# Order of sums, parts and raw loads in the q/k projection of a gated attention and expert kernel

## The chip, the cores and the metric

The kernel runs on one core of a Trainium2 chip. The metric is device time in microseconds (us); the median of three runs of the kernel before is 1882.5 (1881.57 to 1883.23). Engines are named as the profile names them: PE (TensorE), ACT (ScalarE), DVE (VectorE), POOL (GpSimd) and SP (SyncE, which here only issues DMAs). Each engine takes its instructions in its own program order.

## The reference

```
x: (2048, 1024)
gate = sigmoid(sum(x * gate_w))                      # one number a token
a    = attention(x @ wqkv, 32 heads of 32) @ wo
b    = peer(x, w_q, k1, k2, u, v)                    # each of 32 heads picks one of 64 experts
out  = gate * a + (1 - gate) * b
```

All of it is float32. This case touches the first stage: q and k, which are `x @ wqkv` for 2 x 1024 columns, the gate's sums `x * gate_w`, and a fold of `w_q` with the keys that the router of `b` needs.

## The kernel before, in words

**Split products.** A float32 operand is split into a high part (ACT copies it into a rounded type) and a low part (DVE subtracts the high part from it); `split` (L93) does both. A product is then three matmuls for each 128 rows of depth: high x high, high x low, low x high. So whatever PE multiplies must first have gone through ACT and then DVE.

**Two passes, sixteen units.** The tokens are taken in two passes of 1024. A pass has eight units; a unit makes 128 columns of q and 128 of k for the 1024 tokens. The two column blocks and two halves of the depth make a 2 x 2 matrix of weights (A11, A12, A21, A22), the two token blocks and two halves of the depth a 2 x 2 matrix of x (B11 to B22). The first unit of a pass, 0 and 8, is *plain*: eight block products, 96 matmuls, in four PSUM banks (7, 0, 1 and 2). The other seven use seven block products instead of eight (`FACTORS`, L258): P1 = A11 B11, P5 = S1 T1, P6 = S2 T2, P2 = A12 B21, P7 = S3 T3, P3 = S4 B22, P4 = A22 T4, in this order, 12 matmuls each, in banks 0 to 5 in turn. S1 to S4 are sums of weight blocks, made anew for each unit (`w_sum`, L200), T1 to T4 sums of x blocks, made once a pass (`x_sum`, L137). Sums are made on DVE and in place: T1 overwrites raw B11, T3 raw B12, T2 raw B22, T4 raw B21. `w_parts` and `x_quarter` split them. An x sum or split is 128 x 2048 elements ("wide" in what follows), a weight sum, split or evacuation 128 x 512 ("narrow"). The parts of x of a pass also have places that others leave: T2 takes the place of B12's parts, T3 that of raw B22, T4 that of raw B11 and B12 (`PASS`, L101).

**Evacuation.** `evac` (L224) splits a finished block of q or k; later (`run_late`, L215) ACT squares it, which frees the PSUM bank, and issues two stores. The plain units evacuate their four banks while the next unit runs.

**Side work.** `gate_sums` (L173) multiplies all raw x of a pass with the gate's column, 64 PE instructions of 256 columns, copies the four results on ACT into the tile that also holds raw B22, and stores them from POOL's queue. `fold` (L290) multiplies two tiles' worth of `w_q` with key differences (`kpad`), and asks for the next four tiles of 512 KB; after every second fold ACT copies the bank, and in the next unit `fold_t` (L310) transposes the copy on PE, right after P1. It runs at the end of a unit, and in three units after P2 too.

**Order.** All of it stands in the order written out in `unit` (L432): after each product a hook (work put there by name, `hooks`) and then one step of the preparation of the next unit. At the passes' start the order is written out around the plain products (L371 to L404, and L527 to L553) and in `after_plain` (L410). SP issues loads in the order of the program: `load_w` (1 MB, the weights of the unit after the next) at a unit's start, wq tiles at its end, and raw x of the second pass in units 5 and 7 (`next_raw`, L507). Tiles are reused, so a load waits until the last reader of its tile is done, and a store or load also until the transfer that used its semaphore before it is done.

**Unit 15**, the last, splits the router's folded weights between its products (`split_wp`, L586), two buffers deep: the split of one frees the buffer for the load of the one after the next. Router tiles on PE follow it.

Of the kernel before, what the change touches and what calls it, by code (L numbers as in the profile page):

```python
# [31 lines left out]
def gated_mha_peer_kernel(ctx, tc, xT, wqkv, wv, wo, wq, k12, ug, v, out):  # L32
# [81 lines left out]
    def bank_at(i):  # L114
        return ps1.tile([128, 512], F32, name=f"bk{i}")
# [57 lines left out]
    def gate_sums(p):  # L173
        pz = bank_at(6)
        for kc in range(KC):
            for q in range(4):
                nc.tensor.matmul(pz[32 * q:32 * q + 1, :256], gw[:, kc, :], x_raw_at(kc, 256 * q),
                                 start=(kc == 0), stop=(kc == KC - 1))
        for q in range(4):
            row = slice(32 * q, 32 * q + 1)  # L180
            nc.scalar.activation(XR["zs"][row, :], pz[row, :256], AF.Copy)
            c = TOK0[p] + 256 * q
            dma(ZD[:, c:c + 256], XR["zs"][row, :], nc.gpsimd)

# [91 lines left out]
    def load_wq(n):  # L276
        for half in range(2):
            t = wqp.tile([128, 2, 512], F32, name="wqt", bufs=4)
            dma(t, wq[n // 4, n % 4][:, half * 1024:(half + 1) * 1024].rearrange("p (a m) -> p a m", a=2))
            wq_t[n, half] = t  # L280

    def kpad_diffs():
        nc.vector.memset(kpad, 0.0)
        for i in range(4):
            nc.vector.tensor_tensor(out=kpad[:, :, i, 7 * i:7 * i + 7], in0=kraw[:, :, 1:],
                                    in1=kraw[:, :, 0:1].to_broadcast([128, 2, 7]), op=OP.subtract)

    fold_ps, fold_no, pending = [], [0], []

    def fold():  # L290
# [12 lines left out]
        if i == 3:  # L303
            wt = ev.tile([128, 512], F32, name="u4", bufs=1)
            nc.scalar.activation(wt, ps, AF.Copy)
            pending.append((n // 4, wt))
        for m in range(n + 1, min(n + 3, 32)):
            load_wq(m)

    def fold_t():  # L310
        if not pending:
# [55 lines left out]
        nc.tensor.matmul(b0[1, 1][:, :128], ident, ident, start=True, stop=True)  # L367
    dma(gw, ug.rearrange("p (k m) -> p k m", k=KC)[:, :, 64:65], nc.gpsimd)
    dma(kraw, k12.rearrange("p (a e) -> p a e", a=2), nc.gpsimd)

    for kc in range(KC):  # L371
# [35 lines left out]
    def plain_evac(u, w, n):  # L407
        evac(w, CHUNK[u], TOK0[u // KC] // 512 + n, b0[w, n], b0[w, n])

    def after_plain(u, done):  # L410

        rest = [(w, n) for n in range(2) for w in range(2) if (w, n) not in done]
        p, v = u // KC, u + 1
        x_quarter(p, "T2")
        plain_evac(u, *rest.pop(0))
        w_parts(v, "A12")
        plain_evac(u, *rest.pop(0))
        first, second = rest[:1], rest[1:]
        hooks[v, "P1"] = [(plain_evac, u, *a) for a in first] + [(w_parts, v, "S3")]
        hooks[v, "P5"] = [(x_quarter, p, "T3"), (w_parts, v, "A22")]  # L420
        hooks[v, "P6"] = [(x_quarter, p, "T4")] + [(plain_evac, u, *a) for a in second] + [(load_w, u + 3)]

    hooks = {}
    after_plain(0, ())
    load_w(2)
    fold()
    FOLDS = {1, 2, 3, 4, 5, 6, 8, 9, 10, 11, 12, 13}
# [4 lines left out]
    def unit(u):  # L432
        p, c, v = u // KC, CHUNK[u], u + 1
        n0 = TOK0[p] // 512
        seven = v < NUNIT and v != KC
        def ready(name, f=w_parts, *args):
            if seven:
                w_parts(v, name)

        def hook(name):  # L440
            for f, *a in hooks.pop((u, name), []):
                f(*a)

        def place(name):
            return ev.tile([128, 512], F32, name=name, bufs=1)

        def add(out, a, b):
            nc.vector.tensor_tensor(out=out, in0=a, in1=b, op=OP.add)  # L448
# [9 lines left out]
        if seven:  # L458
            w_sum(v, "S1")
            w_sum(v, "S3")  # L460
        ready("A11")
        p5 = product("P5")
        ready("S1")
        if seven:
            w_sum(v, "S2")
        hook("P5")
        p6 = product("P6")
        u2, u4 = place("u2"), place("u4")
        add(u2, c1, p6)
        add(u4, u2, p5)  # L470
        ready("S2")
        if seven:
            w_sum(v, "S4")
# [6 lines left out]
        ready("A12")  # L480
        hook("P2")
        p7 = product("P7")
        u7 = place("u7")
        add(u7, u4, p7)
        add(u2, u2, p7)
        evac(1, c, n0 + 1, u7, p7)
        ready("S3")
        hook("P7")
        p3 = product("P3")
        add(u4, u4, p3)  # L490
        evac(0, c, n0 + 1, u4, p3)
        ready("S4")
        hook("P3")
        p4 = product("P4")
        add(u2, u2, p4)
        evac(1, c, n0, u2, p4)
        ready("A22")
        hook("P4")
        if u in FOLDS:
            fold()  # L500

    def load_a21():
        t = wr.tile([128, 2, KC, 128], F32, name="wraw")
# [3 lines left out]
    def next_raw(which):  # L507
# [4 lines left out]
        else:  # L512
            load_quarter(0 if which == "r21" else 1, 1, XR["B21" if which == "r21" else "B22"])

    hooks[5, "P1"] = [(next_raw, "r21")]
# [12 lines left out]
    load_w(KC + 2)  # L528
    gate_sums(1)
    for ki, n in ((0, 0), (0, 1), (1, 0), (1, 1)):  # L530
        for w in range(2):
            for k in range(HC):
                for i in range(3):
                    plain_mm(w, n, ki * HC + k, i, ki == k == i == 0, ki == 1 and k == HC - 1 and i == 2)
        nxt = KC + 1
        if (ki, n) == (0, 0):
            x_sum(1, "T1")
            x_quarter(1, "T1")
        elif (ki, n) == (0, 1):
            for name in ("S1", "S3"):  # L540
                w_sum(nxt, name)
            w_parts(nxt, "A11")
            w_parts(nxt, "S1")
            w_sum(nxt, "S2")
            w_parts(nxt, "S2")
            for name in ("T3", "T2", "T4"):
                x_sum(1, name)
        elif (ki, n) == (1, 0):
            for w in range(2):
                plain_evac(KC, w, 0)  # L550
            w_sum(nxt, "S4")
            w_parts(nxt, "S4")
    after_plain(KC, ((0, 0), (1, 0)))  # L553
    fold()


# [1116 lines left out]
```

## Time and profile before

| what | us |
|---|---|
| runs of the kernel before, median | 1882.5 |
| the profiled execution, its own time | 1882.36 |
| the span of its profile | 1880.6 |
| opening, up to the first fold on PE | 36.57 |
| router's first tile to the end (starts at) | 413.2 |
| PE busy in the span | 1835.0 |
| DVE busy in the span | 1470.5 |

A timeline row has start, length, engine, line, operation, output<-inputs, shapes and a count; in brackets stand the idle time ahead of it and the instruction that ended it. Rows of equal instructions that follow each other are merged. A name such as `xh` stands for all tiles called xh0, xh1 and so on: `xh`, `xl` and `x` are tiles of x, `A` and `S` parts of weights, `bk` the PSUM banks, `hi` and `lo` the parts of evacuated q and k, `wraw` raw weights, `wqt` raw `w_q`, `wpr` and `wph` the router's weights. PE's row lengths overlap a little, so the distance between starts is the better measure of a product.

### The profile page before, as it was taken

To read this page: it belongs to the slowest core of one execution; us is meant where nothing else is said; L and a number is where in the kernel's file an instruction comes from. 1 tells how busy PE (TensorE), PEld (TensorE's weight loads), DVE (VectorE), ACT (ScalarE), POOL (GpSimd) and SP (SyncE) were. 2 spreads that over 40 slices of the span, in tenths; PEclk is the share of its full clock that TensorE was granted. 3 is DMA by queue.
4 is the path that set the end of the run, shared out by engine and by line. 5 is a ranking of instruction groups with operands and counts; after the bars stand their busy time and mean duration, and the time that the engine had idled before them with its cause. 6 is when DMAs were issued, how large, how long until landed. Compare 5 with 4: busy or idle time off the path is not lost.

```text
span 1880.6 us, 26511 instructions
## 1 busy us (share of the span) xinstructions
PE 1835.0 (98%) x10083; PEld 1106.0 (59%) x10083; DVE 1470.5 (78%) x1276; ACT 1315.2 (70%) x1730; POOL 182.7 (10%) x224
## 2 busy tenths in 40 slices
PE   8799889999999999999999999999999999999999
PEld 6577666777888854444444444444444444447787
DVE  5766486668987878888888888888888888896674
ACT  3544354452143379999999999999999999994221
POOL 0000000006710110000000000000000000000000
PEclk9899989999999999999999999999999999999999
DMA  7587658855027778676777777777877777776861
GB/s 247 184 257 272 218 143 280 295 158 196 2 88 249 257 196 183 155 178 150 174 177 169 172 167 180 166 184 164 186 167 178 156 174 179 172 160 174 290 182 56
DMA packets 136977, 344.98 MB, mean 183 GB/s; under 512 B 18320, under 2 KB 60080, under 8 KB 117712
## 3 DMA queue, kind: packets, MB, share of 16 engines
q1 hardware_dynamic: 97120, 193.41, 34.3%
q0 software_dynamic: 17904, 112.10, 27.7%
q10 hardware_dynamic: 21824, 37.76, 6.5%
q8 instruction: 80, 1.31, 0.3%
q14 instruction: 49, 0.40, 0.1%
HBM read 171.50 MB, written 72.10 MB: 130 GB/s over the span
## 4 chain that ended last, share of the span: by engine, by line
PE 66%; DVE 3%; DMA 3%; POOL 1%; issue 1%; ACT 1%; SPq 0%; DVEq 0%; ACTq 0%; POOLq 0%
PE ring L1220 27%; PE o L1241 25%; PE pa L868 6%; PE bk L868 6%; PE ring L1254 1%; POOL eq L655 1%; DMA accd<-P 1%; DMA out<-rb 1%; DMA accd<-rd 1%; PE pa L1432 1%; DVE eq L664 0%; DMA smd<-ssb 0%; DVE mm L662 0%; DVE vt L95 0%; DVE m L649 0%
## 5 line engine op out<-in xcount | busy, mean ns | idle before, releaser
L1230 ACT ACTIVATE P<-ring 128x1024 f32<-128x1024 f32 (+2 forms) x1031 | 912.6, 985 | 14.7 <-DMA accd<-P 2.2
L1270 DVE TENSOR_TENSOR acc<-acc,P 128x2048 f32<-128x2048 f32 x319 | 731.0, 2291 | 75.1 <-ACT P L1230 49.4
L1241 PE MATMUL o<-P,V 128*32 128x512 f32 x3840 | 464.8, 599 | 0.0
L1220 PE MATMUL ring<-Q,K 98*128 98x512 f32 x1024 | 272.3, 407 | 0.2 <-ACT P L1230 0.2
L1220 PE MATMUL ring<-z,z 98*128 98x512 f32 x1020 | 270.7, 407 | 0.6 <-ACT accd L1230 0.6
L1220 PEld LDWEIGHTS ring<-Q,K 98*128 98x128 f32 x1024 | 181.8, 188 | 144.9 <-ACT P L1230 73.4
L1220 PEld LDWEIGHTS ring<-z,z 98*128 98x128 f32 x1020 | 181.3, 188 | 143.0 <-ACT P L1230 72.3
L1241 PEld LDWEIGHTS o<-P,V 128*32 128x32 f32 x3840 | 98.8, 109 | 223.1 <-issue 213.9
L1263 POOL DMA_DIRECT2D accd<-P x95 | 81.5, 858 | 930.4 <-ACT P L1230 364.0
L1268 DVE TENSOR_TENSOR acc<-P,P 128x2048 f32<-128x2048 f32 x32 | 73.4, 2293 | 73.4 <-ACT P L1230 73.4
L267 PE MATMUL bk<-xh,S 128*128 128x512 f32 x336 | 88.8, 419 | 18.4 <-ACT xh L94 8.9
L267 PEld LDWEIGHTS bk<-xh,S 128*128 128x128 f32 x336 | 67.7, 204 | 36.0 <-ACT xh L94 9.7
L267 PE MATMUL bk<-xl,S 128*128 128x512 f32 x336 | 82.6, 398 | 1.9 <-DVE xl L95 1.8
L267 PE MATMUL bk<-xh,A 128*128 128x512 f32 x336 | 83.0, 396 | 1.1 <-DVE A L95 1.1
L267 PEld LDWEIGHTS bk<-xh,A 128*128 128x128 f32 x336 | 62.0, 188 | 25.2 <-issue 10.1
L94 ACT ACTIVATE hi<-u 128x512 fp32r<-128x512 f32 x42 | 26.5, 632 | 69.4 <-DVE u L448 66.3
L267 PEld LDWEIGHTS bk<-xl,S 128*128 128x128 f32 x336 | 63.6, 191 | 18.0 <-DVE xl L95 2.1
L1273 DVE TENSOR_TENSOR acc<-acc,accd 128x2048 f32<-128x2048 f32 x32 | 73.1, 2285 | 0.0
L1230 ACT ACTIVATE accd<-ring 128x1024 f32<-128x1024 f32 (+2 forms) x64 | 62.3, 1034 | 2.0 <-PE ring L1220 1.9
L868 PE MATMUL pa<-woh,acc 128*128 128x512 f32 x192 | 62.2, 389 | 0.0
L95 DVE TENSOR_TENSOR A<-wraw,A 128x512 fp32r<-128x512 f32 (+2 forms) x47 | 31.3, 667 | 34.3 <-ACT A L94 33.3
L94 ACT ACTIVATE xh<-xh 128x512 fp32r<-128x512 f32 (+1 forms) x25 | 24.2, 986 | 39.5 <-DVE xh L850 20.0
(286 smaller groups left out, 2176.1 us busy)
## 6 DMA issues: line engine op xcount, KB each, us to landing
accd<-P POOLq DMA_DIRECT2D x95, 1024.0 KB, 7.6
wqt<-in_wq SPq DMA_DIRECT2D x64, 512.0 KB
wraw<-in_wqkv SPq DMA_DIRECT2D x28, 512.0 KB
qdh<-hi ACTq DMA_DIRECT2D x32, 256.0 KB
qdl<-lo ACTq DMA_DIRECT2D x32, 256.0 KB
kdh<-hi ACTq DMA_DIRECT2D x32, 256.0 KB
kdl<-lo ACTq DMA_DIRECT2D x32, 256.0 KB
z<-kdh SPq DMA_DIRECT2D x32, 256.0 KB
```

The source lines that it names most:

```text
L94: nc.scalar.activation(hi, src, AF.Copy)
L95: (on or nc.vector).tensor_tensor(out=lo, in0=src, in1=hi.bitcast(F32), op=OP.subtract)
L267: nc.tensor.matmul(ps, a[i][:, k, :], b[j][:, k, :], start=(k == 0 and i == j == 0), stop=(k == HC - 1 and i == 1))
L655: nc.gpsimd.tensor_tensor(out=eq, in0=eq, in1=e8[:, None, :].to_broadcast([128, 64, 8]), op=OP.mult)
L868: nc.tensor.matmul(ps, self.a[a][i][:, k, :], self.b[b][j][k], start=(not first and k == 0 and i == j == 0), stop=(k == HC - 1 and i == 1))
L1220: on_ring(nc.tensor.matmul(ring[:, i, :], K[:98, kt * 128:(kt + 1) * 128], Q[:98, qc * 512:(qc + 1) * 512], start=True, stop=True), i)
L1230: on_ring(nc.scalar.activation(P[h, kt][:, q0 * 512:(q0 + m) * 512].rearrange("p (a m) -> p a m", a=m), ring[:, i:i + m, :], AF.Exp, scale ...
L1241: nc.tensor.matmul(O[h][32 * qc:32 * qc + 32, :], Vt[g][:, kt, 32 * j:32 * j + 32], p[:, qc * 512:(qc + 1) * 512], start=(kt == 0), stop=( ...
L1263: nc.gpsimd.dma_start(ACCD[h], P[h, kt], accum_op=OP.add)
L1268: nc.vector.tensor_add(ACC[h], P[h, 0], P[h, kt])
L1270: nc.vector.tensor_add(ACC[h], ACC[h], P[h, kt])
L1273: nc.vector.tensor_add(ACC[h], ACC[h], ACCD[h])
```

## The change

What it does, in the order of the program:

- The gate's product is cut in two: the half that reads B11 and B12 comes ahead of the fifth of eight plain steps in the first pass (`kc == HC`), the other half ahead of the last; its bank is 5 instead of 6; its copies and stores (`gate_out`) come later, behind S2's parts.
- The key differences `kpad` are made on POOL right after their load, not on DVE in the middle of the plain steps.
- S1, S3 and S1's parts of unit 1 leave the sixth plain step. The preparation at the end of the first pass's plain unit is now T1, T3's sum, S1, S3, A11, T2, S2, gate copies, T4's sum; then A12, one evacuation, T3, S3, and in unit 1 another evacuation, S4, T4, A22 and the last two evacuations.
- In the second unit of a pass (1 and 9) the preparation of the next unit moves from P1 and later to P2 and later, and its A22 into the next unit's P1 (`turns`).
- `load_w` moves from a unit's start to behind P6, and raw x in unit 7 is asked for ahead of it. The fold of unit 6 no longer asks for wq tiles; the start of the second pass does (`load_wqs`).
- In unit 7 the splits of the second pass go B21, B11, B12, A21, B22 instead of B11, B12, A21, B21, B22, and the preparation during the second plain unit is reordered as in the first.
- In unit 15 the eight splits of the router's weights go two, one, one, two, one, one over P1 to P3, instead of one at each and two at P4.

```diff
+    pz = []
+    def gate_mm(kcs):
+        if kcs[0] == 0:
+            pz[:] = [bank_at(5)]
+        for kc in kcs:
             for q in range(4):
...
+    def gate_out(p):
         for q in range(4):
...
     def kpad_diffs():
-        nc.vector.memset(kpad, 0.0)
+        nc.gpsimd.memset(kpad, 0.0)
...
-        if kc == 5:
-            w_sum(1, "S1")
-            w_sum(1, "S3")
-            w_parts(1, "S1")
-            kpad_diffs()
+        if kc == HC:
+            gate_mm(range(HC))
         if kc == KC - 1:
-            gate_sums(0)
+            gate_mm(range(HC, KC))
             x_sum(0, "T1")
             x_quarter(0, "T1")
+            x_sum(0, "T3")
+            for name in ("S1", "S3"):
+                w_sum(1, name)
+            w_parts(1, "S1")
             w_parts(1, "A11")
+            x_sum(0, "T2")
+            x_quarter(0, "T2")
             w_sum(1, "S2")
             w_parts(1, "S2")
-            w_sum(1, "S4")
-            w_parts(1, "S4")
-            for name in ("T3", "T2", "T4"):
-                x_sum(0, name)
+            gate_out(0)
+            x_sum(0, "T4")
...
-    after_plain(0, ())
+    w_parts(1, "A12")
+    plain_evac(0, 1, 0)
+    x_quarter(0, "T3")
+    w_parts(1, "S3")
+    hooks[1, "P1"] = [(plain_evac, 0, 0, 1), (w_sum, 1, "S4"), (w_parts, 1, "S4")]
+    hooks[1, "P5"] = [(x_quarter, 0, "T4"), (w_parts, 1, "A22")]
+    hooks[1, "P6"] = [(plain_evac, 0, 1, 1), (plain_evac, 0, 0, 0)]
...
+        turns = (dict(P2=("S1+", "S3+", "A11"), P7=("S1", "S2+", "S2"), P3=("S4+", "A12"), P4=("S3", "S4"))
+                 if u % KC == 1 else
+                 dict(P1=("S1+", "S3+", "A11"), P5=("S1", "S2+"), P6=("S2", "S4+"), P2=("A12",),
+                      P7=("S3",), P3=("S4",), P4=("A22",)))
...
-        if v + 1 < NUNIT and u % KC != 1 and v + 1 != KC:
-            load_w(v + 1)
...
         hook("P6")
+        ready("P6")
+        if v + 1 < NUNIT and v + 1 != KC:
+            load_w(v + 1)
...
         if u in FOLDS:
-            fold()
+            fold(u != KC - 2)
...
-    hooks[7, "P2"] = [(x_quarter, 1, "B11")]
-    hooks[7, "P7"] = [(x_quarter, 1, "B12")]
-    hooks[7, "P3"] = [(w_parts, 8, "S4", "A21"), (x_quarter, 1, "B21")]
+    hooks[7, "P2"] = [(x_quarter, 1, "B21")]
+    hooks[7, "P7"] = [(x_quarter, 1, "B11")]
+    hooks[7, "P3"] = [(x_quarter, 1, "B12"), (w_parts, KC, "S4", "A21")]
...
     plain_banks(1)
-    load_w(KC + 2)
-    gate_sums(1)
+    load_wqs()
+    gate_mm(range(KC))
+    x_sum(1, "T1")
+    x_quarter(1, "T1")
+    x_sum(1, "T3")
+    run_late()
...
         if (ki, n) == (0, 0):
             for name in ("S1", "S3"):
                 w_sum(nxt, name)
+            w_parts(nxt, "S1")
+            gate_out(1)
+            for name in ("T2", "T4"):
+                x_sum(1, name)
+        elif (ki, n) == (0, 1):
+            x_quarter(1, "T2")
             w_parts(nxt, "A11")
             w_sum(nxt, "S2")
             w_parts(nxt, "S2")
+            x_quarter(1, "T3")
+            w_parts(nxt, "S3")
+            w_sum(nxt, "S4")
+            w_parts(nxt, "S4")
+            x_quarter(1, "T4")
+        else:
+            plain_evac(KC, 1, n)
+            if n:
+                w_parts(nxt, "A12")
+            plain_evac(KC, 0, n)
+    load_w(KC + 2)
...
-    for kc, name in enumerate(("P1", "P5", "P6", "P2", "P7", "P3", "P4")):
-        hooks[15, name] = [(split_wp, kc)]
+    for name, kcs in (("P1", (0, 1)), ("P5", (2,)), ("P6", (3,)), ("P2", (4, 5)), ("P7", (6,)), ("P3", (7,))):
+        hooks[15, name] = [(split_wp, kc) for kc in kcs]
     hooks[15, "P6"].append((split_n1,))
-    hooks[15, "P4"].append((split_wp, 7))
```

More of the change, by code (lines that the diff above doesn't have):

```diff
@@ L171, in x_raw_at @@
         return XR[f"B{1 + kc // HC}{1 + n}"][:, kc % HC, c:c + 256]
-    def gate_sums(p):
-        pz = bank_at(6)
-        for kc in range(KC):
+    pz = []
[3 more added lines that the diff above has]
+        for kc in kcs:
             for q in range(4):
-                nc.tensor.matmul(pz[32 * q:32 * q + 1, :256], gw[:, kc, :], x_raw_at(kc, 256 * q),
+                nc.tensor.matmul(pz[0][32 * q:32 * q + 1, :256], gw[:, kc, :], x_raw_at(kc, 256 * q),
                                  start=(kc == 0), stop=(kc == KC - 1))
+    def gate_out(p):
         for q in range(4):
             row = slice(32 * q, 32 * q + 1)
-            nc.scalar.activation(XR["zs"][row, :], pz[row, :256], AF.Copy)
+            nc.scalar.activation(XR["zs"][row, :], pz[0][row, :256], AF.Copy)
             c = TOK0[p] + 256 * q
@@ L280, in load_wq, with load_wqs, fold @@
             wq_t[n, half] = t
+    def load_wqs():
+        n = fold_no[0]
+        for m in range(n, min(n + 2, 32)):
+            load_wq(m)
     def kpad_diffs():
-        nc.vector.memset(kpad, 0.0)
+        nc.gpsimd.memset(kpad, 0.0)
         for i in range(4):
-            nc.vector.tensor_tensor(out=kpad[:, :, i, 7 * i:7 * i + 7], in0=kraw[:, :, 1:],
+            nc.gpsimd.tensor_tensor(out=kpad[:, :, i, 7 * i:7 * i + 7], in0=kraw[:, :, 1:],
                                     in1=kraw[:, :, 0:1].to_broadcast([128, 2, 7]), op=OP.subtract)
     fold_ps, fold_no, pending = [], [0], []
-    def fold():
+    def fold(load=True):
         for _ in range(2):
@@ L306, in fold @@
             pending.append((n // 4, wt))
-        for m in range(n + 1, min(n + 3, 32)):
-            load_wq(m)
+        if load:
+            load_wqs()
     def fold_t():
@@ L408, in plain_evac @@
         evac(w, CHUNK[u], TOK0[u // KC] // 512 + n, b0[w, n], b0[w, n])
[L410 to L421, printed above, removed]
-    hooks = {}
-    after_plain(0, ())
+    hooks = {}
+    w_parts(1, "A12")
[5 more added lines that the diff above has]
+    hooks[1, "P6"] = [(plain_evac, 0, 1, 1), (plain_evac, 0, 0, 0)]
     load_w(2)
@@ L435, in unit, with ready @@
         seven = v < NUNIT and v != KC
[L436 to L438 removed]
+        turns = (dict(P2=("S1+", "S3+", "A11"), P7=("S1", "S2+", "S2"), P3=("S4+", "A12"), P4=("S3", "S4"))
+                 if u % KC == 1 else
+                 dict(P1=("S1+", "S3+", "A11"), P5=("S1", "S2+"), P6=("S2", "S4+"), P2=("A12",),
+                      P7=("S3",), P3=("S4",), P4=("A22",)))
+        def ready(name):
+            if not seven:
+                return
+            for part in turns.get(name, ()):
+                if part[-1] == "+":
+                    w_sum(v, part[:-1])
+                else:
+                    w_parts(v, part)
         def hook(name):
@@ L457, in unit @@
         hook("P1")
[L458 to L461, printed above, removed]
+        ready("P1")
         p5 = product("P5")
-        ready("S1")
-        if seven:
-            w_sum(v, "S2")
         hook("P5")
+        ready("P5")
         p6 = product("P6")
@@ L479, in unit @@
             fold()
-        ready("A12")
         hook("P2")
+        ready("P2")
         p7 = product("P7")
```

25 lines of the change are left out of this document (9 added, 16 removed).

## The prediction

> **What bounds the kernel now.** I read the windows by stage first, then the TensorE timeline where those show it idle, then the VectorE, ScalarE and SyncE timelines there. The stages are: opening, first pass up to the second folded unit, the rest of that pass, and the same cuts of the second pass.
>
> ```profile
> span 1880.6 us, 26511 instructions
> ...
> 36.57:88.05 51.48, 36.92 (x158) 26.09 (x158) 39.80 (x46) 26.35 (x47) 0.81 (x1) 0.87 0.58 173
> 88.05:208.74 120.69, 120.69 (x578) 90.98 (x577) 71.65 (x111) 49.76 (x105) 2.27 (x3) 1.00 0.82 272
> 208.74:292.80 84.06, 67.06 (x318) 47.75 (x318) 58.80 (x62) 41.92 (x68) 2.78 (x5) 0.88 0.56 175
> ```
>
> The columns are length, busy time of PE, PEld, DVE, ACT, POOL, then granted clock, DMA share and GB/s. From P2 of unit 2 to the end of unit 7 PE is busy all 120.69 us: nothing that other engines do there can be gained. In the two stages after the plain products PE idles 14.6 and 17.0 us and its clock falls to 0.87 and 0.88. Idle time plus slow clock, 14.6 + 0.13 x 36.9 and 17.0 + 0.12 x 67.1, is 44 us: the ceiling of any reordering here. The change lives in these two stages and in unit 15.
>
> ```profile
> 20.38 6.30 PE L255 MATMUL bk<-xl,A 128*128 128x512 f32 x26
> 30.06 1.91 PE L177 MATMUL bk<-xh,gw 128*1 128x256 f32 x32
> ...
> 51.02 0.80 PE L267 MATMUL bk<-xh,S 128*128 128x512 f32 x1 [5.50 <-ACT xh L94]
> 53.54 4.49 PE L267 MATMUL bk<-xh,S 128*128 128x512 f32 x11 [1.73 <-DVE xh L95]
> 66.98 4.82 PE L267 MATMUL bk<-xh,S 128*128 128x512 f32 x12 [6.23 <-ACT bk L222]
> ...
> 82.11 0.62 PE L317 MATMUL bk<-ident,u 128*128 128x128 f32 x4
> 85.33 2.88 PE L267 MATMUL bk<-xh,S 128*128 128x512 f32 x12
> ```
>
> P6 of unit 1 waits for T2's parts, P7 for T3's and for an evacuated bank. A product of 12 matmuls takes 2.72 (85.33 to 88.05), but 4.8 after a long wait: each stall costs some 2 us beyond itself. In the second pass the same comes with waits for raw x, S4, T2 and the fold's copy:
>
> ```profile
> 213.66 0.38 PE L177 MATMUL bk<-xl,gw 128*1 128x256 f32 x2 [1.48 <-DMA xl<-in_xT]
> ...
> 223.94 4.84 PE L255 MATMUL bk<-xh,S 128*128 128x512 f32 x12 [5.44 <-ACT S L94]
> ...
> 256.06 0.80 PE L267 MATMUL bk<-xh,S 128*128 128x512 f32 x1 [3.40 <-ACT xh L94]
> 262.70 2.90 PE L267 MATMUL bk<-xl,A 128*128 128x512 f32 x12
> 285.20 0.66 PE L317 MATMUL bk<-ident,u 128*128 128x128 f32 x4 [2.50 <-ACT u L305]
> 285.61 7.34 PE L267 MATMUL bk<-xh,S 128*128 128x512 f32 x24
> ```
>
> Behind these waits stands one serial chain that crosses DVE and ACT. Its steps:
>
> ```profile
> 32.01 2.29 DVE L142 TENSOR_TENSOR xh<-xh 128x2048 f32<-128x2048 f32 x1 [3.06 <-PE bk L177]
> 37.31 2.29 DVE L95 TENSOR_TENSOR xl<-xh,xl 128x2048 fp32r<-128x2048 f32 x1 [3.01 <-ACT xl L94]
> 44.28 4.68 DVE L142 TENSOR_TENSOR xh<-xh,xh 128x2048 f32<-128x2048 f32 x2
> 54.01 0.68 DVE L95 TENSOR_TENSOR A<-wraw,A 128x512 fp32r<-128x512 f32 x1
> 54.60 0.68 DVE L95 TENSOR_TENSOR lo<-bk,hi 128x512 fp32r<-128x512 f32 x1
> ...
> 33.76 1.57 ACT L181 ACTIVATE xh<-bk 1x256 f32<-1x256 f32 x4 [6.60 <-PE bk L177]
> 35.36 1.92 ACT L94 ACTIVATE xl<-xh 128x2048 fp32r<-128x2048 f32 x1
> 51.48 0.62 ACT L94 ACTIVATE A<-wraw 128x512 fp32r<-128x512 f32 x1
> 52.00 0.59 ACT L94 ACTIVATE hi<-bk 128x512 fp32r<-128x512 f32 x1
> ```
>
> DVE takes 2.2 a wide step and 0.60 a narrow one (54.01 to 54.60); ACT 1.85 and 0.52 to 0.6. DVE began T1's sum only at 32.01, because it overwrites raw x that the gate product, last in PE's order, still had to read; T1's high part then stood behind ACT's four gate copies (3.01 lost); and the sums T3, T2, T4 (44.28 on) stood ahead of T2's parts, which P6 needs first.
>
> **First pass, part by part.** No matmul is added or removed, so what counts is when things come due. I lay the new order out by hand with these steps, each engine in its own order. The gate's first half (16 matmuls of the row at 30.06, which with its second half is 3.5, so 1.75) now runs on PE ahead of the fourth block, 20.4 to 22.15, and frees B11 and B12. S1, S3 and the kpad work leave DVE's queue ahead of the last x splits, so DVE is free at about 22. T1: sum 22.2, high part 24.5, low part done 28.6. T3's sum to 30.8, S1 and S3 to 32.0, their and A11's low parts to 33.3, T2's sum to 35.5 (the second gate half is read by 32.1), its high part to 37.4, low part to 39.6; S2 is whole at 41.4. PE ends the plain products at 20.4 + 4 x 2.72 + 3.5 = 34.8, folds to 36.7 (kpad now comes from POOL, a few small instructions with 15 us and more of cover; were it late, the fold waits), and P1, P5, P6 follow without a stall to 44.9.
>
> Then come new waits. P2 writes bank 0, which needs (1,0) evacuated and squared. On ACT that square stands behind S2, the gate copies (now 40.8 to 42.4), A12, the bank's own split, and T3's high part, which overwrites the tile that holds the gate sums and so waits for their four stores:
>
> ```profile
> zd<-xh POOLq DMA_DIRECT2D x4, 1.0 KB, 1.5
> ...
> 232.24 1.97 POOL L76 DMA_DIRECT2D zd<-xl  x4 [34.14 <-ACT xl L181]
> ```
>
> 0.5 an issue and 1.5 to land put it at 44.6; with S3, c1's copy and the square, bank 0 is free at 48.2. PE waits 3.4 and runs slow: P2 48.2 to 52.7. P7 needs bank 1, squared after T4's high part: 54.7; it ends at 59, P3 62, P4 64.7, fold 66.5, unit 2's P1 69.3. So PE is 12 us ahead there, but DVE isn't: it is busy without a gap from 55 on with four plain evacuations, unit 1's own and all of unit 2's preparation. The fold's copy stands on ACT behind S3 and S4 of that list, at 72.5; unit 2's transposes start at 73.1 (a new stall of 3.8), P5 runs slow to 78.0, P6 ends at 80.8. Before it ended at 88.05. **First pass: -7.2 us.** The bounds: without the new stall at the transposes -11, and -4 if each step of the ACT/DVE chain loses another 0.1 (some 30 steps from 41 to 73).
>
> Moving load_w behind P6 costs nothing: SP doesn't wait for P6, it issues as before once the buffer's last split is done, and only loads in between go first.
>
> **Second pass.** Positions are given on the clock of the profile, that is, without the 7.2 already won.
>
> ```profile
> 201.41 0.63 ACT L94 ACTIVATE hi<-c 128x512 fp32r<-128x512 f32 x1 [4.35 <-DVE c L448]
> 211.25 1.91 ACT L94 ACTIVATE xh<-xh 128x2048 fp32r<-128x2048 f32 x1 [9.22 <-DMA xh<-in_xT]
> ...
> 188.18 2.07 SPq L76 DMA_DIRECT2D wqt<-in_wq  x4
> 193.00 5.74 SPq L76 DMA_DIRECT2D wraw<-in_wqkv  x2
> 198.84 2.07 SPq L76 DMA_DIRECT2D xh<-in_xT  x4
> 202.09 0.38 SPq L76 DMA_DIRECT2D xl<-in_xT  x1
> ```
>
> ACT stood 9.22 in unit 7 for raw x, which was queued behind four wq and two w loads: 5 MB from 188.18 to 211.25, 4.6 us per MB. Now raw x issues when P1 of unit 7 frees its tile (191.9, six products and the transposes before the unit's end at 208.6): 2 MB land at 201, the other 1 MB at 206, w(9) at 210, the wq loads at 219. Meanwhile ACT splits B21, which is long there: 202.0 to 203.9, low part to 206.1. Then, with unit 7's evacuations between: B11 whole at 212.2, B12 218.2, A21 218.8, B22 224.8. PE ends unit 7 at 208.6, finds raw x landed, gate to 212.1, B11 x A11 to 214.9, waits 3.9 for A21 (S4's slot), slow to 223.4, and ends the plain products at 239.6. DVE and ACT, without a gap: T1 whole at 231, S1 235.2, T2 241.8, A11 242.4, S2 244.3, T3 247.7, S3, S4 250.1, T4 253.6, evacuations and A12 257.4. So PE folds to 241.5, P1, P5, P6 to 250.7, then waits 6.7 for A12 and starts P2 at 257.4; before it was 262.70. P2 slow to 262, P7, P3, P4 to 270.3, fold 272.2, P1 of unit 10 275.1. The fold's copy is on ACT at 276.3 by the same count as in unit 2, so transposes start at 277.0 against 285.20. Both are followed by the same slow start. **Second pass: -8.2 us**, bounded by -5.3 (what P2 shows, if the later part of the chain gains nothing) and -12 (if the wait for A12 shrinks to that for S2).
>
> **Unit 15.** The splits of the router's weights move up a slot, two in P1 and P2.
>
> ```profile
> 404.22 0.58 ACT L94 ACTIVATE wph<-wpr 128x448 fp32r<-128x448 f32 x1 [2.86 <-DMA wpr<-wpd]
> 420.55 0.50 PE L641 MATMUL bk<-wph,xl 128*128 128x512 f32 x1 [1.75 <-ACT wph L94]
> 430.82 0.63 DVE L649 TENSOR_REDUCE m<-bk 128x64 f32<-128x448 f32 x1 [1.47 <-ACT xu L645]
> ```
>
> A load lands some 3.6 after the split that frees its buffer, so the sixth and seventh can't come before 416.8 and 417.6: ACT waits there with evacuations queued behind it. The last split comes at 421 instead of 422, PE's first tile gains 2 us, but the last evacuation is 3 later and DVE starts its router steps 1.5 later, which its own 1.47 of idle at 430.82 takes up. I take 0, with -2 and +3.
>
> **Sum**: -7.2 - 8.2 + 0 = -15.4. The profiled execution took 1882.36, its span 1880.6 and 1.76 around it; the median shown is 1882.5, so both agree. 1882.5 - 15.4 = 1867. From unit 2 to the end the work is unchanged and PE busy, so the gain passes through.
>
> **Two rules of the Trainium skill.** The row: after a wait of only 2.50 the next 24 matmuls took 7.34 instead of 5.44 (285.61). The Trainium skill, TensorE: Matmul & The Clock Gate, What's actually happening, says the clock halves only after an idle window of about 3.4 us. By that rule my stalls of 1.9, 3.4 and 3.9 might cost no slow clock, and an estimate from that page is some 4 us more gain, 1863; the trace shows the slow rate, but after shorter waits too, so the sum keeps the rows.
>
> The row for POOL's stores: four issues in 1.97 while DVE ran these:
>
> ```profile
> 231.72 2.29 DVE L95 TENSOR_TENSOR xl<-xl,xl 128x2048 fp32r<-128x2048 f32 x1 [1.73 <-ACT xl L94]
> 233.93 2.29 DVE L142 TENSOR_TENSOR xh<-xh 128x2048 f32<-128x2048 f32 x1
> ```
>
> The Trainium skill, SBUF — State Buffer, two separate sides, speaks against this change: DMAs issued from POOL starve while DVE holds the port pair that they share. That is the third rival.
>
> **Rivals.** (1) *DVE's total sets the end.* The new order only removes idle time ahead of T1, some 6 us (3.06 + 3.01) in the first pass, and PE's lead is paid back in units 2 and 10: half the gain, 1875. For it: DVE had 39.8 of 51.5 busy; against: the chain above already counts DVE without gaps. (2) *Slower: ACT's stores stand behind loads.* ACT's issue of a store waits for the load that last held its semaphore, and what is behind it on ACT waits too, as here in unit 10:
>
> ```profile
> 287.71 0.54 ACT L320 ACTIVATE u<-bk 128x448 f32<-128x448 f32 x1 [1.47 <-DMA wqt<-in_wq]
> ```
>
> In unit 7 two stores stand behind raw x's last piece and the last two wq loads, which are now queued behind raw x. At 4.6 us per MB they land at 206 and 219.5, and ACT gets there at 207.4 and 220.7: 1.3 to spare. At twice that, 9.2 us per MB, the last lands at 247 and B22's split and all behind it come 26 late: 1882.5 - 7.2 - 8.2 + 26 = 1893. It decides from 7.4 us per MB. Against: the rate of 188 to 211 held with stores running too. (3) *POOL's gate stores are held* for a DVE step each: 4 x 2.3 instead of 1.97, T3 7 us later in the first pass; the second has 5 us of room: 1867 + 7 + 2 = 1876. Against: the 1.97. (4) *The transposes don't stall* and the clock recovers: -11 - 12 = 1859.
>
> **Chances.** Forecast 0.58, (1) 0.15, (2) 0.08, (3) 0.07, (4) 0.12. A difference under 0.2%, 3.8 us, can't be told from none here. Slower than that is (2) with 0.01 of (1), 0.09; no change is 0.05 of (1), where PE's whole lead is paid back; faster is the rest, 0.86. The range takes in (4) and (3): 1857 to 1876.
>
> **What would show it.** Right: P6 of unit 1 starts within 0.5 us of P5's end; a wait of 3 to 4 before P2 by a square (bank 0); transposes of unit 2 near 73 with a wait for the fold's copy; gate sums of the second pass without a DMA wait; B21 split while raw x lands; P2 of unit 9 waiting 5 to 8 for A12. Wrong: a store on ACT that waits past 208 on the second pass, T3 more than 3 us behind the gate copies, or PE idle in units 2 to 7.

## The result, and the profile after

The changed kernel takes 1871.27 us (median of five, 1868.22 to 1874.19) against 1882.5 (median of five, 1879.4 to 1883.96): ratio 0.9942, 95% interval 0.9926 to 0.9958. The gain is 11.2 where 15.4 was forecast. Run again beside other kernels it took 1870.59 against 1883.61, ratio 0.9932 (0.9918 to 0.9945). The profiled execution is the fastest of its five, 1868.22 with a span of 1866.5, so its span shows 14.1 of gain, 3 more than the medians.

The windows by stage of the changed kernel (length, busy time of PE, PEld, DVE, ACT, POOL, then granted clock, DMA share, GB/s). The first starts at P1 of unit 1 (the one before started a fold earlier; from P1 it was 49.63 long), the second at P2 of unit 2, the third at the second gate sum and ends at P2 of unit 10:

```profile
36.67:82.62 45.95, 35.09 (x144) 26.10 (x141) 32.98 (x42) 25.70 (x49) 2.78 (x5) 0.89 0.70 210
82.62:203.65 121.03, 121.03 (x578) 91.00 (x577) 75.37 (x113) 53.64 (x110) 2.27 (x3) 1.00 0.80 265
203.65:280.79 77.14, 63.15 (x317) 46.03 (x317) 54.32 (x58) 38.19 (x64) 2.78 (x5) 0.91 0.60 182
```

Between the two passes PE is still busy throughout, 121.03 of 121.03. Where it idled, the old waits are gone and others stand in other places, less in sum: 10.9 instead of 14.6 in the first stage, 14.0 instead of 17.0 in the third. The third stage is 6.9 shorter, so more than half of that, 3.9, are matmuls that ran faster (granted clock 0.91 instead of 0.88). PE's timeline of the changed kernel, first pass:

```profile
42.90 3.04 PE L272 MATMUL bk<-xh,S 128*128 128x512 f32 x12 [0.46 <-ACT xh L186]
49.21 3.02 PE L272 MATMUL bk<-xl,A 128*128 128x512 f32 x12 [3.27 <-ACT bk L227]
55.80 5.49 PE L272 MATMUL bk<-xh,S 128*128 128x512 f32 x12 [3.57 <-ACT bk L227]
...
75.18 1.12 PE L327 MATMUL bk<-ident,u 128*128 128x128 f32 x4 [3.55 <-ACT u L315]
75.95 4.12 PE L272 MATMUL bk<-xl,S 128*128 128x512 f32 x12
```

P6 starts half a microsecond behind P5's end (it stood 7.2 before). P2 and P7 now wait for squares of the banks that they write, the transposes of unit 2 for the fold's copy. The second pass of the changed kernel, same view:

```profile
203.65 1.91 PE L180 MATMUL bk<-xh,gw 128*1 128x256 f32 x32
...
211.89 0.73 PE L260 MATMUL bk<-xh,S 128*128 128x512 f32 x2 [1.67 <-ACT S L94]
214.30 4.14 PE L260 MATMUL bk<-xh,S 128*128 128x512 f32 x10 [1.67 <-DVE S L95]
...
253.10 5.49 PE L272 MATMUL bk<-xl,A 128*128 128x512 f32 x12 [6.80 <-ACT A L94]
...
274.82 0.66 PE L327 MATMUL bk<-ident,u 128*128 128x128 f32 x4 [2.84 <-ACT u L315]
275.24 5.72 PE L272 MATMUL bk<-xh,S 128*128 128x512 f32 x24
```

The gate sum no longer waits for raw x; A21 costs 3.3 in two pieces, A12 6.80. Starts of the same steps on PE in six profiled executions (the last two kernels come below):

| kernel | P2 of unit 2 | P4 of unit 7 | P2 of unit 10 | P4 of unit 15 | router's wait for DVE | span |
|---|---|---|---|---|---|---|
| before | 88.05 | 205.92 | 292.78 | 410.33 | 470.31 | 1880.6 |
| changed | 82.62 | 200.83 | 280.79 | 398.33 | 457.16 | 1866.5 |
| first pass only | 83.87 | 201.73 | 288.86 | 406.59 | 468.01 | 1879.2 |
| second pass only | 87.59 | 206.45 | 287.73 | 405.29 | 466.66 | 1876.3 |
| all reordered | 70.78 | 196.91 | 266.37 | 386.37 | 445.32 | 1855.6 |
| the same, stores on POOL | 68.99 | 188.21 | 254.94 | 376.91 | 434.08 | 1845.6 |

In the changed kernel 5.4 comes up to unit 2, nothing (118.2 against 117.9) up to unit 7, 6.9 up to unit 10, nothing up to unit 15, 1.1 in the router; behind it 1409.3 follow against 1410.3. Of the 5.4, 1.8 stand before the first fold on PE already (it starts at 34.81 against 36.57), and that start varies by 2.3 from run to run, as the last section shows.

### The profile page after: what moved, and what is told of

Its sections match the earlier page's. It is cut to its first block, busy times and chain, and to the rows that moved or that the text cites. A ratio compares the mean times of both kernels' runs of the same rounds, so it can differ in the third digit from the quotient of the medians.

```text
span 1866.5 us, 26507 instructions
## 1 busy us (share of the span) xinstructions
PE 1827.8 (98%) x10083; PEld 1105.7 (59%) x10083; DVE 1467.8 (79%) x1271; ACT 1316.1 (71%) x1730; POOL 183.7 (10%) x229
## 4 chain that ended last, share of the span: by engine, by line
PE 64%; issue 6%; DVE 2%; POOL 2%; DMA 1%; ACT 0%; POOLq 0%; DVEq 0%; ACTq 0%; SPq 0%
PE ring L1239 28%; PE o L1260 25%; PE pa L887 6%; PE pa L1444 2%; PE ring L1273 1%; POOL eq L674 1%; PE pa L1451 1%; DVE eq L683 0%; DVE mm L681 0%; DMA t1l<-xl 0%; DVE m L668 0%; DVE xh L893 0%; DMA vd<-xh 0%; DMA xl<-in_wo 0%; DVE m L669 0%
## 5 line engine op out<-in xcount | busy, mean ns | idle before, releaser
L1239 PEld LDWEIGHTS ring<-Q,K 98*128 98x128 f32 x1024 | 182.0, 188 | 144.0 <-ACT P L1249 73.1
L272 PE MATMUL bk<-xh,S 128*128 128x512 f32 x336 | 83.0, 400 | 4.0 <-ACT bk L227 3.6
L272 PEld LDWEIGHTS bk<-xh,S 128*128 128x128 f32 x336 | 64.2, 193 | 19.1 <-ACT bk L227 4.0
L1292 DVE TENSOR_TENSOR acc<-acc,accd 128x2048 f32<-128x2048 f32 x32 | 73.1, 2284 | 0.0
L272 PE MATMUL bk<-xl,A 128*128 128x512 f32 x168 | 43.1, 408 | 10.1 <-ACT A L94 6.8
```

The lines of the kernel that those rows point to most:

```text
L272: nc.tensor.matmul(ps, a[i][:, k, :], b[j][:, k, :], start=(k == 0 and i == j == 0), stop=(k == HC - 1 and i == 1))
L1239: on_ring(nc.tensor.matmul(ring[:, i, :], K[:98, kt * 128:(kt + 1) * 128], Q[:98, qc * 512:(qc + 1) * 512], start=True, stop=True), i)
L1292: nc.vector.tensor_add(ACC[h], ACC[h], ACCD[h])
```

## The experiments

**One pass at a time.** The second pass alone (everything up to unit 6 as before), then the first alone (everything from unit 7 on as before):

```diff
-        if kc == HC:
-            gate_mm(range(HC))
+        if kc == 5:
+            w_sum(1, "S1")
+            w_sum(1, "S3")
+            w_parts(1, "S1")
...
```
```diff
-    load_wqs()
+    load_w(KC + 2)
     gate_mm(range(KC))
-    x_sum(1, "T1")
...
+    gate_out(1)
...
```

> Only the first pass is as changed (gate sum in two halves, the new order of sums and parts, unit 1's turns, kpad from POOL, weights asked for behind P6 up to unit 6); unit 7, its loads, the second pass and unit 15 are as before. Theory (the two passes gain apart from each other, each by the order in which ACT and DVE make its operands): P6 of unit 2 ends near 82.6 as in the changed kernel, 5.4 before the old 88.05, nothing is lost up to the end, 1882.5 - 5.4 = 1877. Rival (DVE's total decides and the lead is paid back in the units behind): 0, 1882. Rival (all of the 11 to 14 us comes from raw x being there earlier in the second pass): 0, 1882.

> Only unit 7 with its loads, the second pass and its turns are as changed; the first pass and unit 15 are as before. Theory: the distance from the end of unit 7 to P2 of unit 10 shrinks from 84.0 to 77.1, so -6.9, 1875.6. Rival (the second pass gains only because the first hands it a lead): 0, 1882. Rival (what the first pass gains is given back and the second pass makes all of it): -12, 1870.

Measured: 1878.77 (ratio 0.9982, 0.9973 to 0.9991) and 1876.31 (0.9966, 0.9957 to 0.9976) against 1882.55: -3.8 and -6.2. The table shows each lead arise in its own pass and last up to P4 of unit 15 (3.7 and 5.0 there). Behind it the router's stretch differs from run to run: of the first pass's lead the span of its profile, the slowest of eleven runs, keeps 1.4. Neither is a condition of the other, and neither is the whole: together they make 10.0, without unit 15.

**Unit 15 as before.**

```diff
-    for name, kcs in (("P1", (0, 1)), ("P5", (2,)), ("P6", (3,)), ("P2", (4, 5)), ("P7", (6,)), ("P3", (7,))):
+    for kc, name in enumerate(("P1", "P5", "P6", "P2", "P7", "P3", "P4")):
...
```

> The changed kernel, but unit 15's splits of the router's weights in the slots of before. Theory (unit 15's part is worth what lies between the end of P4 of unit 15 and the row where PE waits for DVE in the router: 57.1 before, 55.95 after): +1.1, 1872.4. My forecast had 0 for it, 1871.3. Rival (the spread of these runs hides it): within 0.5 of the changed kernel.

Measured 1873.38 (0.9945, 0.9932 to 0.9959), 2.1 and 2.8 above the changed kernel's two medians. From P4 of unit 15 to the router's wait it takes 59.67 (399.41 to 459.08), against 58.83 with the change. The intervals of the ratios overlap (0.9945 against 0.9942 and 0.9932), so the times alone don't settle it; the positions are on the side of a gain of 1 to 2, not of my 0.

**Raw x not ahead.**

```diff
+        if u == KC - 1:
+            load_w(v + 1)
...
-            fold(u != KC - 2)
+            fold()
...
-    load_wqs()
```

> The changed kernel, but the loads around unit 7 are in the order of before: wq behind unit 6's folds and w of unit 9 at unit 7's start, both ahead of raw x. Everything else stays, B21's split first among it. Theory (raw x ahead of the others is worth part of the second pass's gain): in the old order the gate sum stood 1.5 for raw x's last MB and the first of its splits began 2.5 past unit 7's end, against 1 ahead of it in the changed kernel, so gate and all splits behind come 3.5 to 5 later: 1875 to 1876. Rival (the splits of B21 fill the wait and DVE's later work is the bound, so the load is hidden): 0 to +1, 1871 to 1872. Rival (the loads ahead are the whole gain of the second pass): +6.9, 1878.

Measured 1876.18 (0.9964, 0.995 to 0.9977), +4.9. ACT of this kernel in unit 7, and PE in its gate sum:

```profile
196.11 1.90 ACT L94 ACTIVATE xl<-x 128x2048 fp32r<-128x2048 f32 x1
...
206.70 1.91 ACT L94 ACTIVATE xh<-xh 128x2048 fp32r<-128x2048 f32 x1 [4.49 <-DMA xh<-in_xT]
```
```profile
204.47 0.61 PE L180 MATMUL bk<-xh,gw 128*1 128x256 f32 x8 [0.52 <-DMA xh<-in_xT]
206.67 0.61 PE L180 MATMUL bk<-xh,gw 128*1 128x256 f32 x8 [1.59 <-DMA xh<-in_xT]
...
209.55 0.39 PE L180 MATMUL bk<-xl,gw 128*1 128x256 f32 x2 [1.85 <-DMA xl<-in_xT]
```

B21's split still fills part of the wait, but B11's begins at 206.70 against 202.86 and the gate sum loses 4.0. So most of the second pass's gain hangs on the order of loads, as expected.

**The gate in one piece.**

```diff
-        if kc == HC:
-            gate_mm(range(HC))
...
-            gate_mm(range(HC, KC))
+            gate_mm(range(KC))
```

> The changed kernel, but the gate sum of the first pass is in one piece behind the last x splits, as before (same place as its second half now). Theory (T1's sum may start at 22.2 only because the first half of the gate sum has read B11 and B12 by then): T1's sum starts near 32 and the whole chain on DVE moves by 9.8 less the 3 to 4 that DVE idles in it, so +6, 1877: the first pass's gain is lost. Rival (the gain lies in the order of sums and parts, the gate's halves add nothing that PE sees): 0 to +1, 1871 to 1872.

Measured 1878.85 (0.9983, 0.9973 to 0.9993), +7.6: the first pass's whole gain and more. Its DVE:

```profile
29.48 2.29 DVE L142 TENSOR_TENSOR xh<-xh 128x2048 f32<-128x2048 f32 x1 [7.59 <-PE bk L180]
33.76 2.29 DVE L95 TENSOR_TENSOR xl<-xh,xl 128x2048 fp32r<-128x2048 f32 x1 [1.98 <-ACT xl L94]
```

T1's sum stands 7.59 for the gate and starts at 29.48, not at 22.23, and P2 of unit 2 starts at 90.26. With the sums in their new order and the gate in one piece there is nothing left to gain in the first pass (the second keeps its gain: 80.73 from P4 of unit 7 to P2 of unit 10): the first half of the gate, 16 matmuls of the program moved ahead, carries the pass.

**Transposes behind P6, in units 2 and 10.**

```diff
-        fold_t()
+        if u % KC != 2:
+            fold_t()
...
         p6 = product("P6")
+        fold_t()
```

> The changed kernel, but in units 2 and 10 the fold's transposes stand behind P6 on PE instead of behind P1; nothing else moves. PE waits 3.55 and 2.84 there for the fold's copy, and the matmuls behind run slow for 1.2 and 0.1. Theory (only the fold's copy is late there; the operands of P5 and P6 of these units are whole by 73.2 and 278, so nothing takes the wait's place): -3.55 - 1.2 - 2.84 - 0.1 = -7.7, 1863.6. Rival (DVE's total decides: PE waits for other operands of the same unit instead): 0 to -2, 1869 to 1871.

Measured 1867.94 (0.9924, 0.991 to 0.9938; 1866.99 to 1873.52): -3, between the two. The profile is of its slowest run, 5.6 above the median, and shows where the rest goes in that run; the others were not profiled. Units 2 and 10 run through up to P2 without a wait for the fold's copy; the fold at the end of unit 10 then waits 1.5 for wq tiles. And in unit 4 stand ACT, and with it PE:

```profile
118.71 0.34 ACTq L76 DMA_DIRECT2D qdl<-lo  x1
119.10 0.63 ACT L94 ACTIVATE A<-wraw 128x512 fp32r<-128x512 f32 x1 [3.57 <-DMA wqt<-in_wq]
119.64 0.58 ACT L315 ACTIVATE u<-bk 128x512 f32<-128x512 f32 x1
```
```profile
120.27 1.11 PE L327 MATMUL bk<-ident,u 128*128 128x128 f32 x4 [4.99 <-ACT u L315]
```

A store that ACT issues waits for a wq load, the fold's copy stands behind it, PE behind the copy. That is the mechanism of my second rival, in a place that I hadn't named: PE runs ahead, and the next store meets a load that is still under way.

**Another order of the chain, both passes.** T3's sum ahead of T1's low part and T4's ahead of T2's, so that DVE works while ACT splits; gate copies earlier; squares of banks 0 and 1 ahead of parts that P2 and P7 don't read. In its second pass one block product of unit 8 takes unit 9's A11 and two take its A12, so only the first pass is read.

```diff
             x_sum(0, "T1")
+            x_sum(0, "T3")
             x_quarter(0, "T1")
...
+            gate_out(0)
             x_sum(0, "T2")
+            x_sum(0, "T4")
             x_quarter(0, "T2")
...
```

> The changed kernel with another order of sums and parts in both passes: T3's sum ahead of T1's low part and T4's ahead of T2's (DVE stood 2 us for ACT at each), gate copies ahead of T2's high part, squares of banks 0 and 1 ahead of what P2 and P7 don't read, A11 ahead of T2 and A12 and bank 0 ahead of T4 in the second pass. The transposes of units 2 and 10 stay where they are. By the same steps laid out by hand unit 1 ends some 9 and unit 9 some 11 earlier. Theory (waits between ACT and DVE set unit 1 and 9, not DVE's busy time; from 55 on DVE has some 4 of idle left to lose beside the 4 to 6 saved ahead of it): half of it lasts, -4 to -5 a pass, 1862. Rival (DVE's total decides, the lead is paid back at the transposes): 0 to -2, 1869 to 1871.

Measured 1882.11 (0.9995, 0.9986 to 1.0004), not the 1862 that I expected: all of the loss is in the second pass, where plain products wait 9.95 and 8.43 for unit 9's weights. In the first pass of this kernel PE is done with unit 1 8.6 sooner (its fold starts at 58.10 against 66.72), and then:

```profile
72.25 1.11 PE L327 MATMUL bk<-ident,u 128*128 128x128 f32 x4 [9.22 <-ACT u L315]
73.02 5.41 PE L272 MATMUL bk<-xl,S 128*128 128x512 f32 x12
...
80.99 2.88 PE L272 MATMUL bk<-xl,A 128*128 128x512 f32 x12
```

P2 of unit 2 comes at 80.99, 1.6 sooner than in the changed kernel: 7 of the 8.6 are paid back at the transposes (counted from each kernel's first fold, unit 1 ends 9.9 and P2 starts 2.9 sooner). There my first rival is right in its effect: a lead of PE in unit 1 is worth only what the fold's copy allows.

**Low parts behind the sums, in units 1 and 9.**

```diff
-        split(hi, lo, src)
+        nc.scalar.activation(hi, src, AF.Copy)
+        lows.append(lambda: nc.vector.tensor_tensor(out=lo, in0=src, in1=hi.bitcast(F32), op=OP.subtract))
...
+            run_low()
```

`run_low` stands behind the `w_sum` calls of the slot and ahead of its `w_parts`.

> The changed kernel, but in units 1 and 9 the low part of an evacuation comes on DVE behind the sums of the same slot instead of straight behind the add (where DVE waits 0.44 to 0.76 for ACT's high part, 3.7 in six places from 60.9 to 74.2). Theory (these waits, which my forecast had left out, are why the first pass gained 5.4 and not 7.2): two of the six go, -1 to -1.5 a pass, 1868 to 1869. Rival (ACT's order or PE sets that stretch, the waits are slack): 0, 1871.

Measured 1865.47 of four runs (0.9907, 0.9892 to 0.9922): three at 1865.2 to 1865.7, and the profiled one at 1872.62; the median is 3 below the 1868 to 1869 expected. In the profiled run the distance from P2 to the transposes is 19.1 in the second pass (256.23 to 275.31) against 21.7 in the changed kernel (21.3 to 21.6 in five other profiles of that order): -2.6, more than the 1.0 to 1.5 expected.

```profile
256.23 5.20 PE L282 MATMUL bk<-xl,A 128*128 128x512 f32 x12 [6.79 <-ACT A L94]
...
275.31 0.66 PE L337 MATMUL bk<-ident,u 128*128 128x128 f32 x4 [0.86 <-ACT u L325]
```

DVE's waits for ACT in this stretch fall from 4.1 (3.7 in two of the others) to 1.6, so the distance shrinks by about what they do. In its first pass the last of these low parts comes 22.2 behind P2 of unit 1 instead of 23.8 (at 72.82; 73.03 in the changed kernel). Then a store stands again, for a wq load, and takes more than was won:

```profile
75.56 0.46 ACTq L76 DMA_DIRECT2D qdl<-lo  x1
76.06 0.63 ACT L94 ACTIVATE S<-S 128x512 fp32r<-128x512 f32 x1 [2.66 <-DMA wqt<-in_wq]
```

**All of it, with stores on ACT and on POOL.** The three last kernels' edits together, A11 and A12 of unit 9 split only where the plain products have read the old ones. Then with POOL issuing the stores, in this kernel and in the changed one, and the changed one again.

```diff
-            late.append((dma, dst[128 * c:128 * c + 128, n * 512:(n + 1) * 512], t, nc.scalar))
+            late.append((dma, dst[128 * c:128 * c + 128, n * 512:(n + 1) * 512], t, nc.gpsimd))
```

> The changed kernel with the transposes of units 2 and 10 behind P6, low parts of evacuations behind the sums of their slot in units 1 and 9, and the other order of sums and parts of both passes, in the second pass without taking A11 and A12 of the next unit before the plain products have read the old ones. By hand PE is 13 us ahead at the end of unit 2 and 8 in unit 10. Theory (the chain between ACT and DVE sets the end of both stages): -8 to -10, 1861 to 1863. Rival (PE's lead past some 5 us is paid back in units 3 to 7, because stores on ACT stand behind wq loads that are asked for as late as before, as in the profile with the transposes behind P6): -3 as there, 1868.

> The changed kernel, but the stores of q and k parts are issued by POOL instead of ACT. Theory (in the changed kernel ACT stands at such a store where nothing waits for it, 4.15 at raw x's first piece): 0, 1871, and ACT's waits for a load at L330 and at L94 are gone. Rival (ACT's issues and their waits are part of what makes units 2 and 10 late): -2 to -4, 1867 to 1869. Rival (POOL's issues are held up while DVE runs): stores late, their tiles come free late, +3 and more.

> The kernel with all of the reorderings, and with the stores of q and k parts issued by POOL. Theory (stores on ACT behind wq loads take back a part of the lead): faster than the same kernel with its stores on ACT, by 2 to 4. Rival (loads alone are late: PE waits for wq itself): the same within 1.

> The changed kernel once more, beside the others on the same chip: 1871.3 if its spread (1868.2 to 1874.2) is the same here; and whether P2 of unit 1 runs at full clock (3.0) behind its wait of 3.2 to 3.4 or slow (5.5), as both were seen with the same work.

Measured, in one set with before at 1883.61: 1856.82 with all of it (0.9854, 0.9839 to 0.9869), faster than theory and rival had it; 1848.17 with stores on POOL too (0.9815, 0.9801 to 0.9828), 8.7 less where I expected 2 to 4; the changed kernel with stores on POOL 1874.85 (0.9956, 0.9942 to 0.9969), and the changed kernel again 1870.59. Waits of ACT between 60 and 200 in the kernel with all of it and stores on ACT (total, times, longest):

```profile
ACT A L94 <- DMA wqt<-in_wq: 6.2, 3, 2.9
ACT u L340 <- DMA xh<-in_xT: 4.1, 1, 4.1
```

With POOL none of ACT's waits between 60 and 200 is for a load, and of the 10.0 by which the two spans differ 6.9 lie between P2 of unit 2 and P4 of unit 7 (126.13 against 119.22 by the table). The windows of that kernel, the same three stages:

```profile
36.67:68.99 32.32, 30.40 (x144) 23.14 (x141) 26.79 (x35) 19.81 (x39) 8.67 (x16) 1.00 0.78 268
68.99:191.02 122.03, 121.67 (x579) 91.07 (x577) 79.10 (x119) 55.79 (x117) 26.58 (x48) 1.00 0.83 277
191.02:254.94 63.92, 59.40 (x318) 44.03 (x317) 50.58 (x52) 34.70 (x59) 13.04 (x25) 0.97 0.57 200
```

PE is busy 30.4 of 32.3 and 59.4 of 63.9, and the clock hardly falls. In the changed kernel the same edit of the queue loses 4.3 instead (1874.85 against 1870.59), where my theory had 0. That is the size that I had named for issues held up by DVE, but they aren't held up: of 115 issues of these stores between 60 and 400, 112 take 0.54 and none over 0.57. In its profile a fold waits for its wq tiles (0.94 and 0.93, at 365.47 and 367.46) and takes 5.0 instead of 1.9. SP asked for these tiles at 354.28, in the changed kernel's second profile at 354.24, so they were asked for no later and landed later; why wasn't tried. The two profiled runs are only 0.5 apart, so this fold needn't be all of the 4.3.

## Why the prediction was right, and where it was off

*What bounds the kernel.* Right. The two stages gain apart from each other, and nothing changes from unit 2 to 7 and from unit 10 to 15.

*First pass, up to P2.* The hand-made order held to a few tenths. Forecast against trace: T1's sum 22.2 and 22.23, end of the plain products 34.8 and 34.81, S2's low part whole 41.4 and 42.1, P2's wait 3.4 and 3.27. That the end of the plain products agrees to 0.01 is luck, as the start of the fold behind them varies by 2.3 from run to run. P2 started 1.0 late, because T3's high part began at 45.64 instead of 44.6: S2 waited 0.70 for ACT, and the gate's four stores took a median of 2.6 to land, not 1.5. P2 ran at full clock, 3.02 instead of the 4.5 that I had put down; over eight profiles it took 3.0 to 5.5 (last section), so the 3.02 is this run's luck.

*First pass, sum.* -7.2 forecast, -5.4 in this pair; over seven profiles P2 of unit 2 starts at 87.8 in the two with the old first pass and at 83.4 in the five with the new one (82.62, 83.87, 83.42, 82.29, 85.02), so -4.4. Counted from each kernel's first fold it is -3.6 (51.5 and 52.4 against 47.6 to 49.2). The mis-sized step is that DVE "is busy without a gap from 55 on". DVE of the changed kernel:

```profile
60.88 0.69 DVE L95 TENSOR_TENSOR lo<-c,hi 128x512 fp32r<-128x512 f32 x1 [0.70 <-ACT hi L94]
...
65.80 0.69 DVE L95 TENSOR_TENSOR S<-S,S 128x512 fp32r<-128x512 f32 x1 [0.44 <-ACT S L94]
...
67.85 0.69 DVE L95 TENSOR_TENSOR S<-wraw,S 128x512 fp32r<-128x512 f32 x1 [0.76 <-ACT S L94]
...
69.84 0.69 DVE L95 TENSOR_TENSOR lo<-u,hi 128x512 fp32r<-128x512 f32 x1 [0.70 <-ACT hi L94]
...
73.03 0.69 DVE L95 TENSOR_TENSOR lo<-u,hi 128x512 fp32r<-128x512 f32 x1 [0.69 <-ACT hi L94]
...
74.16 0.69 DVE L95 TENSOR_TENSOR S<-S,S 128x512 fp32r<-128x512 f32 x1 [0.44 <-ACT S L94]
```

Six waits, 3.7 together: a low part follows straight behind the add that makes its source, and ACT's copy lies between. The transposes stand at 75.18 instead of 73.1. Not all of these 2.1 come from the six waits: P2 was 1.0 late and P7 1.1 (55.80 against 54.7) before them, behind a handover of the same kind, S2's, and the gate's stores. My forecast gives no single steps between 55 and 72.5, so it doesn't show what took up the rest of the 3.7; its lower bound of -4, 0.1 more a step, is near what was measured. Taking some of these waits out won 2.6 in the second pass, so they are on the path there; in the first pass a store covered it.

*Second pass.* -8.2 forecast; -6.9 in this pair. From P4 of unit 7 to P2 of unit 10 it takes 87.0 in the two profiles with the old order (86.86, 87.13) and 80.7 in five with the new one (79.96, 81.28, 80.67, 80.73, 80.62), so -6.3. Right were the gate sum without a wait, B21 split ahead of raw x (at 196.85), and the wait for A12, 6.7 and 6.80. Off is the same step: P2 of unit 9 to the transposes took 21.7, where I had 277.0 - 257.4 = 19.6, and DVE's waits for ACT there are 4.1. In this pair 1.6 came back at once, as the 24 matmuls behind took 5.72 instead of 7.34; that varies from run to run too (7.38 with raw x not ahead).

*Unit 15.* 0 forecast; -1.1 in this pair, and over eight profiles 60.6 from P4 of unit 15 to the router's wait with the old splits (59.98, 61.42, 61.37, 59.67) against 58.7 (58.83, 58.52, 58.87, 58.60). I held that ACT would stand for the sixth and seventh load and that the last evacuation would come later. It doesn't stand: ACT splits them at 399.69 and 403.02 without a wait, PE's wait of 1.75 for split weights (420.55 before) is gone, and a longer one for a bank takes its place, before and changed:

```profile
413.67 0.50 PE L641 MATMUL bk<-wph,xh 128*128 128x512 f32 x1 [0.46 <-ACT bk L222]
```
```profile
403.16 0.50 PE L660 MATMUL bk<-wph,xh 128*128 128x512 f32 x1 [1.95 <-ACT bk L227]
```

DVE reaches its router steps 12.9 sooner (411.92 against 424.78), 0.9 more than the 12.0 that PE was ahead at P4 of unit 15.

*Sum.* -4.4 - 6.3 - 1.9 = -12.6 by these means (-11.8 with the first pass counted from the first fold). The medians show -11.2 and -13.0. The passes fell short of the forecast by 2.8 and 1.9; unit 15, where I had 0, made up 1.9 of that, which is luck.

*Rivals.* The first (DVE's total) holds for part of it: what PE wins in unit 1 beyond the fold's copy is lost. Not because DVE is full, though: with all of the reorderings P2 of unit 2 starts 11.8 sooner, with the same work. The second (stores behind loads) didn't come in the place that I named: between 208 and 300 ACT's longest wait for a load is 0.6. One came earlier, where ACT waited 4.15 for a piece of raw x; nothing was lost, because ACT's next work, at 196.31, waited 3.46 for DVE anyway:

```profile
191.86 0.34 ACTq L76 DMA_DIRECT2D kdl<-lo  x1
192.30 0.55 ACT L330 ACTIVATE u<-bk 128x448 f32<-128x448 f32 x1 [4.15 <-DMA xh<-in_xT]
```

It is what holds up the faster kernels behind unit 2, and POOL's queue takes it away there. The third (POOL's gate stores held by DVE) didn't come: the four issues took 1.98 from 41.94 on, with T4's sum running at 42.03. Of the fourth, the clock recovered in two places, but the transposes stalled.

## What to carry to other kernels

Where one serial chain feeds PE, look first for the one reader that holds the chain's first step back: here half of a small product, moved ahead, carried a whole pass. Lay the new order out engine by engine, and count the latency of each handover (here 0.4 to 0.8 where a step follows straight behind its source on another engine) beside the busy times. And before an engine is made to run ahead, look at what its neighbours issue: a store queued behind a load pays the lead back some units later, out of sight of the stage that was mended.

## What was not expected of the hardware

*The clock behind a wait.* P2 of unit 1 is the same 12 matmuls behind nearly the same wait in eight profiles:

| wait, us | 3.15 | 3.19 | 3.20 | 3.26 | 3.27 | 3.27 | 3.35 | 3.47 |
|---|---|---|---|---|---|---|---|---|
| P2, us | 3.01 | 3.06 | 4.62 | 5.49 | 3.02 | 5.49 | 5.49 | 4.41 |

So the length of a wait doesn't by itself decide whether PE runs slow behind it, and shorter waits go both ways too: 24 matmuls behind 2.84 took 5.72 in the changed kernel and 7.38 in the one with raw x not ahead. The Trainium skill, TensorE: Matmul & The Clock Gate, What's actually happening, says that the clock halves after an idle window of about 3.4 us and that the window runs freely; that the same wait goes both ways agrees with a free-running window, slow matmuls behind 2.50 (before) and 2.84 don't agree with its length.

*The opening's spread.* The first fold on PE starts between 34.65 (raw x not ahead) and 36.94 (transposes behind P6) in eight profiles of kernels with the same opening, behind waits of up to 0.9 for the first x splits. These 2.3 are there before any step that the kernels differ in. They are part of the spread between runs of one kernel: of the two profiles of the changed kernel the later one starts its first fold 1.0 later (35.83 against 34.81), and its span is 4.6 longer.
